# Joining two of the four exponentials of an attention step into one ScalarE instruction over two neighbouring PSUM banks

## The chip, the cores and the metric

The kernel runs on one core of one Trainium2 chip. The metric is the device time of one execution in microseconds, taken as the median of several runs. A core has a matrix engine (TensorE, in the profile PE, with its weight loads under PEld), a vector engine (VectorE, DVE), an engine for activation functions (ScalarE, ACT), a general engine (GpSimd, POOL) and an engine that mostly issues transfers (SyncE, SP). Matmuls write into PSUM, which has eight banks; one bank holds a tile of 128 rows by 512 fp32 numbers. ScalarE and VectorE read PSUM; GpSimd and the DMA queues do not.

## The reference

One block of a model: a layer norm without weights, an attention over 2048 tokens with 32 heads of 16 numbers each, a two-layer network with a tanh-approximated gelu on the same normed input, and a gated sum.

```
xn = layernorm(x)                        # x: 2048 x 512
q, k, v = split(xn @ wqkv)               # 32 heads of 16
p = softmax(q @ k.T * 16 ** -0.5)        # per head, 2048 x 2048
s = (p @ v) @ wo
h = gelu(xn @ w1 + b1)                   # 2048 x 1376
g = silu(h @ w2 + b2)
out = x + s * g
```

## The kernel before, in words

Most of the work is the attention. The kernel never stores the 2048 x 2048 scores of a head. It computes them twice. The first time (**S** operations) a tile of scores stands with the queries on the partitions, and VectorE takes the maximum of each row out of it (`s_mm`, `s_max`, L191). The second time (**T** operations, `t_one`, L715) it stands transposed, with the keys on the partitions, and the row maximum is subtracted inside the matmul by two extra rows of the operands; ScalarE takes the exponential out of PSUM into an SBUF tile (L717). A third matmul (`pv_step`, **V** in the order strings, L781) multiplies the exponentials by the values. To save precision, fp32 operands are split in a high and a low part; that is why the S operands have 48 rows (three pieces of 16) and the T operands 50.

An operand of 48 or 50 rows fills less than half of TensorE's 128 rows. So operands lie either in partitions 0 and up (row side 0, `a = 0`) or in partitions 64 and up (row side 1, `a = 1`), and two matmuls of different sides can run at the same time.

The work is cut in 32 units: 8 groups of 4 heads, times 4 chunks of 512 queries. A unit has 16 steps, one for each 128 keys. One step `n` (unit `ua`, key block `ka`) does for its 4 heads:

- four T matmuls and four exponentials, 128 x 512 each (T0 to T3 below);
- three S tiles, that run ahead of the T work by some units: two whole ones (`S`, the first on side 0, the next on side 1), and one tile written in two halves of 256 columns, `X` on side 0 and later `Y` on side 1, with a wait of TensorE's queue ahead of `Y` until `X` is done, since two row sides must not write one bank together. Each of the three gets one VectorE reduction;
- the V matmuls of the step before: 8 instructions, four column tiles in two passes each.

The order inside a step is written out by hand and kept by every engine's queue (`manual_schedule`): each letter issues its instructions in turn. A full step (three S tiles, `want == 3`) uses `TSXTTSTYV`, except `STXTTSTYV` at `ka` 0 and `XTSTTYSTV` at `ka` 2. There are 490 full steps, `n` 2 to 491; after them come 21 with no S (`TTTTV`), which also hold output work (`w_halves`, L905), and two odd ones at the start. Ahead of all this lies a first phase with the layer norm, the projections and the feed-forward network, into which the first S tiles are mixed.

PSUM has these users in a full step. The S ring (`ps_a`, `ps_b`, `ps_x`) has three banks that are handed round: S and X take the first one in the ring and put it at the end (X only when Y is issued). The T tiles rotate over `ps_m` and the three buffers of `ps_t` (`t_tile`). `ps_v` collects a unit's V result over 16 steps. At the end of a unit VectorE copies `ps_v` into SBUF (L788, tile `os`), which is issued behind the V of `ka` 0 of the next unit; the V of `ka` 1 writes `ps_v` anew. For two units at a time (later one) the maxima are turned by a TensorE transpose (`s_end1`, L268) into a T bank, copied out by VectorE (L278), and written to DRAM, from where they come back as the two extra rows of T.

Steps that the change and the prediction touch: `t_one` and `t_tile` (banks, row side, exponential), `pv_step` (the copy at L788), `s_end1` (the bank of the transpose), the order strings `ORDER` and `AFTER`, and the bank choice of the first phase and of the output (`a_tile`, `quad`, `down`, `w_mul`).

Of the kernel before, what the change touches and what calls it, by code (L numbers as in the profile page):

```python
# [8 lines left out]
F32 = mybir.dt.float32  # L9
F32R = mybir.dt.float32r  # L10
AF = mybir.ActivationFunctionType
OP = mybir.AluOpType
AX = mybir.AxisListType
PSUM = bass.MemoryType.PSUM
DRAM = bass.MemoryType.DRAM

P = 128
S = 2048
D = 512
# [3 lines left out]
NT = S // P  # L23
CH = 512
NCH = S // CH
# [5 lines left out]
SCALE = DH ** -0.5  # L31
VW = DH + 1
LEAD = 144
NW = 10
# [3 lines left out]
APART = 5  # L38
HB = 4
W2B = 2  # L40
ORDER = {0: "TTTTV", 3: "TSXTTSTYV"}
AFTER = {0: "STXTTSTYV", 2: "XTSTTYSTV"}
HC = CH // 2
PAIRED = 28
KB = 3
# [5 lines left out]
def fused(ctx: ExitStack, tc: tile.TileContext, x, wqk, wv, wo, w1, b1, w2, b2, out):  # L51
    nc = tc.nc
# [3 lines left out]
    ps_a = ctx.enter_context(tc.tile_pool(name="ps_a", bufs=1, space=PSUM))  # L56
    ps_b = ctx.enter_context(tc.tile_pool(name="ps_b", bufs=1, space=PSUM))
    ps_x = ctx.enter_context(tc.tile_pool(name="ps_x", bufs=1, space=PSUM))
    ps_t = ctx.enter_context(tc.tile_pool(name="ps_t", bufs=3, space=PSUM))
    ps_v = ctx.enter_context(tc.tile_pool(name="ps_v", bufs=1, space=PSUM))  # L60
    ps_m = ctx.enter_context(tc.tile_pool(name="ps_m", bufs=1, space=PSUM))

# [25 lines left out]
    SYNC = mybir.DependencyInfo(mybir.DependencyClass.Sync, mybir.DependencyReason.DATA)  # L88
    qss = []
    NU = NG * NCH  # L90

    s_ring = [ps_a, ps_b]

    def s_tile(held=False):
        pool = s_ring.pop(0)
        if not held:
            s_ring.append(pool)
        return pool.tile([P, CH], F32, name="ps"), pool
# [164 lines left out]
    prog = {}  # L263

    def s_end1(u):
        pm = s_tile()[0] if "seen" in prog or u == NU - 1 else t_tile()
        n = 2 * GH * NCH * len(units_of(u))
        nc.tensor.matmul(pm[:n, :P], NM.pop(u).rearrange("p u i a -> p (u i a)"), ident_r, start=True, stop=True)  # L268
        MH[u] = pm
# [122 lines left out]
    with ExitStack() as s1:  # L392
# [4 lines left out]
        def a_tile(shape):  # L397
            banks[0] += 1
            i = banks[0] % 6
            if i < 3:  # L400
                return (ps_a, ps_b, ps_x)[i].tile(list(shape), F32, name="ps")
            return ps_t.tile(list(shape), F32, name="pst")


        xs, xns = {}, {}
# [197 lines left out]
    PH = {}  # L603
# [21 lines left out]
    def down(c, f, part):  # L625
        i = c * FT + f
        if f == 0 and part == 0:
            PA[c] = [ps_v.tile([P, D], F32, name="pv")] + [ps_t.tile([P, D], F32, name="pst") for t in range(3)]
        h, w = HS[c, f], W2[c, f]
        side = (part + i) % 2  # L630
        ops = [[], []]
        for a in range(2):
            for t in ((0, 1), (2, 3))[(a + side) % 2]:
                ts = slice(t * P, (t + 1) * P)
                for n, (x, y) in enumerate(((0, 0), (0, 1), (1, 0))):
                    ops[a].append(((c, t), PA[c][t], h[x][:, ts], w[y],
                                   f == 0 and part == 0 and n == 0, f == FT - 1 and part == 1 and n == 2))
        run(ops)
        if part == 0:
            w2_split(i + 1)  # L640
            w2_load(i + 3)
            return
        del HS[c, f], W2[c, f]
        if f == FT - 1:
            for t in (0, 2, 1, 3):
                gt = wk.tile([P, D], F32, name="gt", bufs=4)
                if c == NCH - 1:
                    nc.vector.tensor_add(gt, PA[c][t], b2_sb)  # L648
                else:
                    nc.scalar.activation(gt, PA[c][t], AF.Copy)  # L650
                rs = slice(c * CH + t * P, c * CH + (t + 1) * P)
                if c < NCH - 1:
                    chores.append((gt, rs))
                else:
                    nc.gpsimd.dma_start(g_d[rs, :], gt)
# [22 lines left out]
    def quad(n, at):  # L678
        us = first[n]
        for u, b in zip(us, BANKS[n]) if at == 0 else ():  # L680
            pool, name = {"x": (ps_x, "ps"), "m": (ps_m, "ps"), "v": (ps_v, "pv"), "t": (ps_t, "pst")}[b]
            PH[u] = pool.tile([P, CH], F32, name=name)
        for i in range(at, at + 2):
            hooks = {}
            if n == VQ - 2 and i in (0, 2):
                hooks[3] = [lambda: w1_split(0) if i == 0 else w1_load(1)]
            run((terms(us[i], 0, i < 2), terms(us[(i + 2) % 4], 1, i < 2)), hooks)
            if i >= 2:
                for u in (us[i - 2], us[i]):
                    v_out(u[1] * NCH + u[2], PH.pop(u))  # L690
# [4 lines left out]
            errands.append((load_k, g, (i,)))  # L695

    PT = {}
    turns, PN = [0], []

    def t_tile():  # L700
        turns[0] += 1
        if turns[0] < 5:
            pool = (ps_m, ps_x, ps_a, ps_b)[turns[0] - 1]
        else:
            pool = ps_m if turns[0] % 4 == 1 else ps_t
        return pool.tile([P, CH], F32, name="pst" if pool is ps_t else "ps")

    def t_one(u, k, p, a):
        g = u // NCH
        if (u, k) not in PT:  # L710
            PT[u, k] = slot(3 + len(PN) % 3, (P, GH, CH))
            PN.append(1)
        ps = t_tile()
        r = slice(64 * a, 64 * a + 3 * DH + 2)
        nc.tensor.matmul(ps, kts[g % KB][p][r, k * P:(k + 1) * P],  # L715
                         QT[u][r, p, :], start=True, stop=True)
        nc.scalar.activation(PT[u, k][:, 2 * p + a, :], ps, AF.Exp, scale=SCALE)  # L717

    k_ones(kts[0])
    for n, e in enumerate(plan):  # L720
        if e[0] == "half":
            half(*e[1:])
        elif e[0] == "first":
            quad(*e[1:])
            if e[1:] == (0, 2):
                ask_qs(1)
        else:
            if e[1] == parts[-2]:
                nc.scalar.activation(mhw, ident_r[:1, :1].bitcast(F32), AF.Exp)
            if e[1] == parts[-1]:  # L730
                for i in range(EARLY):
                    t_one(0, 0, i // 2, i % 2)
            down(*e[1])
        if e == ("first", VQ - 1, 2):
            w2_split(0)
            w2_load(2)
            ask_k(1)
        if e[0] == "half" and pairs[e[1]][0] == ("q", NG - 1, 0) and e[2] == 1:
            kts.append([slot(p, (P, S), F32R) for p in range(2)])
            kws.append(None)  # L740
            qss.append(slot(2, (P, 2, 2, CH), F32R))
            ask_k(2)
        if n == len(plan) - 8:
            load_qt(0)
            load_mh(0)
# [29 lines left out]
    def pv_step(u, k):  # L775
        g = u // NCH
        if k == 0:
            PV[u] = ps_v.tile([P, CH], F32, name="pv")
        for j in range(GH):
            h = (g * GH + j) * VW  # L780
            nc.tensor.matmul(PV[u][32 * j:32 * j + 32, :], vsb[:, k, h:h + 32], PT[u, k][:, j, :],  # L781
                             start=(k == 0), stop=(k == NT - 1))
        del PT[u, k]
        if k == NT - 1:
            OS[u] = wb.tile([P, CH], F32, name="os", bufs=1)
            pv = PV.pop(u)
            if u < NU - 1:
                nc.vector.tensor_copy(OS[u], pv)  # L788
            else:
                nc.scalar.activation(OS[u][:, :HC], pv[:, :HC], AF.Copy)  # L790
                nc.vector.tensor_copy(OS[u][:, HC:], pv[:, HC:])
# [76 lines left out]

    def w_mul(t, ks, parts=(0, 1)):
        if t not in PW:  # L870
            PW[t] = [ps_t.tile([P, CH], F32, name="pst") if NW <= t < NT - NCH or i else
                     ps_m.tile([P, CH], F32, name="ps") if t == NT - 1 else s_tile()[0]
                     for i, cs in enumerate(cols(t))]
        for i, cs in enumerate(cols(t)):
            if i in parts:
                for k in ks:
                    mm3(PW[t][i][:, :cs.stop - cs.start], OTS[t, k], (wo_h[:, k, cs], wo_l[:, k, cs]),
                        k == 0, k == KT - 1)
# [97 lines left out]
    for n in range(L + 1):  # L976
        ua, ka = divmod(n, 16)
        want = due(n) - due(n - 1)
        i = 0
        for u in list(ended):  # L980
            if u >= PAIRED or ka > 2 and since.setdefault(u, n) < n:
                s_end0(u)
        order = ORDER[want] if n > 1 else ("TTTTV", "TTSTSVT")[n]
        if want == 3 and ua:
            order = AFTER.get(ka, order)
        for op in order:
            if op in "SXY":
                s_op(op)
            elif op == "V":
                if n:  # L990
                    pv_step(*divmod(n - 1, 16))
                for _ in range(4):
                    tick()
                flush()
            else:
                if EARLY <= 4 * n + i < 4 * L:
                    t_one(ua, ka, i % 2, 1 - i // 2)
                for f, args in todo.get((n, i), []):
                    f(*args)
                i += 1  # L1000
# [54 lines left out]
```

## Time and profile before

| | |
|---|---|
| median of 3 runs | 1565.8 us (1565.47 to 1566.19) |
| the profiled execution's own time | 1565.5 us |
| its span, first to last instruction | 1563.7 us |
| granted TensorE clock | 1.000 |
| first phase, to the first V | 470.39 us |
| the 490 full steps | 1007.94 us |
| steps after them, to the last V | 62.13 us |

How to read it: a busy time is the union of an engine's instruction times. An instruction's recorded time includes the way through its pipeline, so two instructions in a row overlap: four exponentials of about 0.60 us each follow one another at less than 0.50 us. An engine can therefore look busy without a gap and still have been held up; the distance from start to start tells more. "Idle before" names what ended an engine's idle time, and for a wait on several semaphores that is a guess.

### The profile page before, as it was taken

The numbers are of one execution on the slowest core, as the hardware profiler recorded it, in microseconds if no ns is written. First come the engines' busy times: TensorE is split into PE (matmuls) and PEld (weight loads), VectorE is DVE, ScalarE is ACT, GpSimd is POOL, SyncE is SP. The second block draws the span as 40 slices with busy tenths as digits, with TensorE's granted clock in tenths as the row PEclk, the third lists the DMA queues.
The fourth block names the chain that finished last, engine by engine and source line by source line (L and its number), as shares of the span: only waits on it lengthen the run. The fifth ranks groups of instructions, "written<-read, shape, count | busy, mean of one in ns | idle before, by whom it ended". The sixth has DMA issues, their size and how long they took to land.

```text
span 1563.7 us, 31870 instructions
## 1 busy us (share of the span) xinstructions
PE 1556.6 (100%) x12264; PEld 951.5 (61%) x12264; DVE 1416.1 (91%) x2290; ACT 1234.5 (79%) x2397; POOL 371.7 (24%) x394
## 2 busy tenths in 40 slices
PE   9999999999999999999999999999999999999998
PEld 7899999999994444444444444444444444444455
DVE  7599999999999999999999999999999999999834
ACT  4333333434349999999999999999999999999984
POOL 4145575756640011001100100100010000000143
PEclk9999999999999999999999999999999999999999
DMA  6626343454322113111511411321151111110163
GB/s 209 153 60 158 116 139 100 155 145 136 124 91 60 40 42 61 29 38 44 86 24 28 70 41 32 59 44 29 26 79 27 33 29 33 40 30 22 46 197 115
DMA packets 74648, 116.87 MB, mean 75 GB/s; under 512 B 23013, under 2 KB 24293, under 8 KB 73321
## 3 DMA queue, kind: packets, MB, share of 16 engines
q1 hardware_dynamic: 70748, 101.89, 23.9%
q0 software_dynamic: 3264, 12.35, 4.7%
q8 instruction: 97, 1.59, 0.4%
q10 hardware_dynamic: 484, 0.60, 0.1%
q14 instruction: 55, 0.44, 0.1%
HBM read 84.35 MB, written 25.97 MB: 71 GB/s over the span
## 4 chain that ended last, share of the span: by engine, by line
PE 98%; DVE 1%; ACT 0%; DMA 0%; issue 0%; DVEq 0%
PE pv L781 33%; PE pst L715 20%; PE ps L589 13%; PE ps L185 11%; PE pst L589 7%; PE ps L715 7%; PE pv L589 2%; PE ps L905 1%; PE ps L82 1%; PE ps L459 1%; PE pst L82 1%; DVE st L418 0%; PE pst L441 0%; DMA xt<-in_x 0%; PE pst L459 0%; ACT slot L717 0%
## 5 line engine op out<-in xcount | busy, mean ns | idle before, releaser
L191 DVE TENSOR_REDUCE mx<-ps 128x2 f32<-128x512 f32 x2048 | 1317.9, 687 | 87.2 <-PE ps L185 44.4
L717 ACT ACTIVATE slot<-pst 128x512 f32<-128x512 f32 x1533 | 826.0, 603 | 12.8 <-PE pst L715 7.0
L781 PE MATMUL pv<-slot,vsb 128*32 128x512 f32 x4096 | 545.4, 605 | 0.3 <-DVE os L788 0.3
L715 PE MATMUL pst<-qt,kt 50*128 50x512 f32 x1149 | 378.8, 430 | 0.5 <-DVE gt L648 0.3
L185 PE MATMUL ps<-kt,slot 48*128 48x512 f32 (+1 forms) x1364 | 377.1, 368 | 0.0
L715 PEld LDWEIGHTS pst<-qt,kt 50*128 50x128 f32 x1149 | 192.3, 185 | 252.5 <-ACT slot L717 235.9
L717 ACT ACTIVATE slot<-ps 128x512 f32<-128x512 f32 x515 | 310.9, 604 | 1.8 <-PE ps L185 0.7
L185 PEld LDWEIGHTS ps<-kt,slot 48*128 48x128 f32 x1364 | 226.6, 184 | 39.4 <-DVE mx L191 35.4
L589 PE MATMUL ps<-slot,w1h 64*128 64x512 f32 x1088 | 218.4, 393 | 0.0
L185 PE MATMUL ps<-kt,qz 48*128 48x512 f32 x512 | 201.8, 394 | 0.0
L185 PE MATMUL ps<-slot,slot 48*128 48x512 f32 (+1 forms) x598 | 165.3, 366 | 0.0
L715 PE MATMUL ps<-qt,kt 50*128 50x512 f32 x387 | 160.6, 417 | 0.0
L589 PEld LDWEIGHTS ps<-slot,w1h 64*128 64x128 f32 x1088 | 151.9, 186 | 10.5
L589 PE MATMUL ps<-slot,w1l 64*128 64x512 f32 x544 | 148.4, 393 | 0.0
L781 PEld LDWEIGHTS pv<-slot,vsb 128*32 128x32 f32 x4096 | 81.0, 108 | 98.9 <-issue 90.4
L378 POOL TENSOR_TENSOR hl<-hg,hh 128x512 fp32r<-128x512 f32 x76 | 96.8, 1296 | 151.9 <-ACT hh L377 113.9
L251 POOL CAST nmh<-nm 128x16 fp32r<-128x16 f32 x32 | 6.3, 197 | 519.4 <-DVE nm L248 418.0
L371 ACT ACTIVATE hg<-ps,b_sb 128x512 f32<-128x512 f32 x44 | 27.9, 684 | 125.2 <-PE ps L589 100.4
L715 PE MATMUL pst<-qt,slot 50*128 50x512 f32 x384 | 112.5, 416 | 0.0
L185 PEld LDWEIGHTS ps<-slot,slot 48*128 48x128 f32 x598 | 99.1, 184 | 16.4 <-DVE mx L191 15.1
L715 PEld LDWEIGHTS ps<-qt,kt 50*128 50x128 f32 x387 | 71.3, 185 | 41.8 <-ACT slot L717 36.0
L185 PEld LDWEIGHTS ps<-kt,qz 48*128 48x128 f32 x512 | 94.0, 184 | 0.5
(165 smaller groups left out, 1722.6 us busy)
## 6 DMA issues: line engine op xcount, KB each, us to landing
raw<-in_w SPq DMA_DIRECT2D x88, 256.0 KB
qk_h<-hh SPq DMA_DIRECT2D x32, 256.0 KB
qk_l<-hl SPq DMA_DIRECT2D x32, 256.0 KB
qt<-qk_h SPq DMA_DIRECT2D x128, 64.0 KB
slot<-qk_h SPq DMA_DIRECT2D x92, 64.0 KB
g_d<-gt POOLq DMA_DIRECT2D x16, 256.0 KB, 3.4
qt<-qk_l SPq DMA_DIRECT2D x64, 64.0 KB
dn<-den_d SPq DMA_DIRECT2D x32, 128.0 KB
```

Source lines behind the costliest of these rows:

```text
L82: nc.tensor.matmul(ps, lhs[a], rhs[b], start=first and n == 0, stop=last and n == 2)
L185: return nc.tensor.matmul(ps[:, c0:c0 + w], QS[u][r, p, qi * P:(qi + 1) * P], kts[u // NCH % KB][p][r, k0:k0 + w], start=True, stop=True).ins
L191: nc.vector.tensor_reduce(MX[u][:, 2 * p:2 * p + 2, qi, ki][:, heads, parts], ps.rearrange("p (n c) -> p n c", c=HC), axis=AX.X, op=OP.max)
L251: nc.gpsimd.tensor_copy(hl[:, 0], nm)
L371: nc.scalar.activation(raw, ph.pop(u), AF.Gelu_apprx_tanh, bias=b1_sb[:, u[2]:u[2] + 1])
L378: nc.gpsimd.tensor_sub(hl, raw, hh.bitcast(F32))
L459: nc.tensor.matmul(pq["q", g, c], W1[g][i][:, k * P:(k + 1) * P], (xh, xl)[j][c][:, k], start=n == 0 and k == 0, stop=n == 2 and k == KT - 1)
L589: i = nc.tensor.matmul(ps, lhs[r], rhs[r], start=first, stop=last).ins
L715: nc.tensor.matmul(ps, kts[g % KB][p][r, k * P:(k + 1) * P], QT[u][r, p, :], start=True, stop=True)
L717: nc.scalar.activation(PT[u, k][:, 2 * p + a, :], ps, AF.Exp, scale=SCALE)
L781: nc.tensor.matmul(PV[u][32 * j:32 * j + 32, :], vsb[:, k, h:h + 32], PT[u, k][:, j, :], start=(k == 0), stop=(k == NT - 1))
L905: HALF[0] = nc.tensor.matmul(PW[i][0], OTS[i, k][x][r], (wo_h, wo_l)[y][r, k], start=k == 0 and side == 0 and n == 0, stop=k == KT - 1 and ...
```

## The change

- The three `ps_t` buffers become one tile of two neighbouring banks (`two_t`, pool `ps_p`) and one single bank. `t_bank(i)` gives bank 0 or 1 of the pair, or the single one (2); without an argument it goes round the three. The places that took `ps_t` in the first phase and at the end take it from there.
- In full steps T1 goes to bank 0 and T2 to bank 1 of the pair, T0 to the single bank, T3 to `ps_m`. After T2, one ScalarE instruction takes the exponential of both banks, 128 x 1024, into the two neighbouring parts of the SBUF tile. T0 and T3 keep their own. For this the heads and row sides of the four T change: the sides were 1, 1, 0, 0 and are now 1, 0, 1, 0 (`SIDES`).
- All full steps use the order `XTSTTYSTV`.
- The copy of a unit's V result (L788) moves from VectorE to ScalarE, behind the last exponential of `ka` 0.
- The transpose of the maxima takes a bank of the S ring in place of a T bank.

```diff
-ORDER = {0: "TTTTV", 3: "TSXTTSTYV"}
-AFTER = {0: "STXTTSTYV", 2: "XTSTTYSTV"}
+ORDER = {0: "TTTTV", 3: "XTSTTYSTV"}
+SIDES = ((1, 1), (0, 0), (0, 1), (1, 0))
...
-    ps_t = ctx.enter_context(tc.tile_pool(name="ps_t", bufs=3, space=PSUM))
+    ps_t = ctx.enter_context(tc.tile_pool(name="ps_t", bufs=1, space=PSUM))
+    ps_p = ctx.enter_context(tc.tile_pool(name="ps_p", bufs=1, space=PSUM))
...
+    two_t = ps_p.tile([P, 2, CH], F32, name="two_t")
+    spare = [0]
+
+    def t_bank(i=None):
+        if i is None:
+            i = spare[0] % 3
+            spare[0] += 1
+        return two_t[:, i] if i < 2 else ps_t.tile([P, CH], F32, name="pst")
...
-        pm = s_tile()[0] if "seen" in prog or u == NU - 1 else t_tile()
+        pm = s_tile()[0]
...
-            PA[c] = [ps_v.tile([P, D], F32, name="pv")] + [ps_t.tile([P, D], F32, name="pst") for t in range(3)]
+            PA[c] = [ps_v.tile([P, D], F32, name="pv")] + [t_bank(i) for i in (0, 2, 1)]
...
-    def t_one(u, k, p, a):
+    def t_one(u, k, i, pair=False):
         g = u // NCH
+        p, a = SIDES[i]
...
-        ps = t_tile()
+        if u == k == 0:
+            ps = (ps_m, ps_x, ps_a, ps_b)[i].tile([P, CH], F32, name="ps")
+        elif i == 3:
+            ps = ps_m.tile([P, CH], F32, name="ps")
+        else:
+            ps = t_bank((i + 2) % 3)
...
-        nc.scalar.activation(PT[u, k][:, 2 * p + a, :], ps, AF.Exp, scale=SCALE)
+        if not pair or i in (0, 3):
+            nc.scalar.activation(PT[u, k][:, 2 * p + a, :], ps, AF.Exp, scale=SCALE)
+        elif i == 2:
+            nc.scalar.activation(PT[u, k][:, :2], two_t, AF.Exp, scale=SCALE)
...
-                nc.vector.tensor_copy(OS[u], pv)
+                nc.scalar.activation(OS[u], pv, AF.Copy)
...
-            PW[t] = [ps_t.tile([P, CH], F32, name="pst") if NW <= t < NT - NCH or i else
+            PW[t] = [t_bank(2 if t == NW else t == NW + 1) if NW <= t < NT - NCH or i else
...
-        if want == 3 and ua:
-            order = AFTER.get(ka, order)
...
-                    t_one(ua, ka, i % 2, 1 - i // 2)
+                    t_one(ua, ka, i, want == 3)
```

More of the change, by code (lines that the diff above doesn't have):

```diff
@@ L401, in a_tile @@
                 return (ps_a, ps_b, ps_x)[i].tile(list(shape), F32, name="ps")
-            return ps_t.tile(list(shape), F32, name="pst")
+            b = t_bank()
+            return b.rearrange("p (a b) -> p a b", b=shape[-1]) if len(shape) > 2 else b
         xs, xns = {}, {}
@@ L680, in quad @@
         for u, b in zip(us, BANKS[n]) if at == 0 else ():
-            pool, name = {"x": (ps_x, "ps"), "m": (ps_m, "ps"), "v": (ps_v, "pv"), "t": (ps_t, "pst")}[b]
-            PH[u] = pool.tile([P, CH], F32, name=name)
+            if b == "t":
+                PH[u] = t_bank()
+            else:
+                pool, name = {"x": (ps_x, "ps"), "m": (ps_m, "ps"), "v": (ps_v, "pv")}[b]
+                PH[u] = pool.tile([P, CH], F32, name=name)
         for i in range(at, at + 2):
@@ L697, in fused @@
     PT = {}
[L698 to L706, printed above, removed]
-    def t_one(u, k, p, a):
+    PN = []
+    def t_one(u, k, i, pair=False):
         g = u // NCH
+        p, a = SIDES[i]
         if (u, k) not in PT:
@@ L712, in t_one @@
             PN.append(1)
-        ps = t_tile()
+        if u == k == 0:
+            ps = (ps_m, ps_x, ps_a, ps_b)[i].tile([P, CH], F32, name="ps")
+        elif i == 3:
+            ps = ps_m.tile([P, CH], F32, name="ps")
+        else:
+            ps = t_bank((i + 2) % 3)
         r = slice(64 * a, 64 * a + 3 * DH + 2)
@@ L731, in fused @@
                 for i in range(EARLY):
-                    t_one(0, 0, i // 2, i % 2)
+                    t_one(0, 0, i)
             down(*e[1])
```

## The prediction

> **What bounds the kernel now.** I read the page first, for the engines and for the chain that ended last; then busy time by stage; then the timeline of single steps.
>
> ```profile
> PE 1556.6 (100%) x12264; PEld 951.5 (61%) x12264; DVE 1416.1 (91%) x2290; ACT 1234.5 (79%) x2397; POOL 371.7 (24%) x394
> ...
> PE 98%; DVE 1%; ACT 0%; DMA 0%; issue 0%; DVEq 0%
> ```
>
> The chain runs through TensorE nearly throughout. A gain must shorten what TensorE does or waits for; ScalarE time as such is worth nothing. The stage table (length, then busy time and count of PE, PEld, DVE, ACT, POOL) and the same stretch cut down to the V matmuls, the L278 copies and the L788 copies:
>
> ```profile
> 470.39:1478.33 1007.94, 1007.84 (x7856) 476.68 (x7855) 950.57 (x1567) 999.79 (x1961) 75.97 (x127) 1.00 0.20 41
> 470.39:1478.33 1007.94, 522.16 (x3920) 77.36 (x3921) 1.00 0.20 41
> 470.39:1478.33 1007.94, 3.56 (x13) 1.00 0.20 41
> 470.39:1478.33 1007.94, 20.44 (x30) 1.00 0.20 41
> ```
>
> 3920 V instructions, 8 to a step: 490 full steps of 2.057 us on average, with 13 transposes of maxima and 30 unit ends. All three engines look full, so the start times must tell. Two steps, each from T0 to the next T0 (start, length, instruction):
>
> ```profile
> 803.91 1.57 ACT L717 ACTIVATE slot<-pst 128x512 f32<-128x512 f32 x3
> 804.89 0.49 PE L715 MATMUL ps<-qt,slot 50*128 50x512 f32 x1
> 805.42 0.60 ACT L717 ACTIVATE slot<-ps 128x512 f32<-128x512 f32 x1
> 805.53 0.18 PEld L715 LDWEIGHTS pst<-qt,slot 50*128 50x128 f32 x1
> 805.91 1.57 ACT L717 ACTIVATE slot<-pst 128x512 f32<-128x512 f32 x3
> 805.95 1.07 PE L781 MATMUL pv<-slot,vsb 128*32 128x512 f32 x8
> 806.95 0.50 PE L715 MATMUL ps<-qt,slot 50*128 50x512 f32 x1
> 806.95 0.50 PE L185 MATMUL ps<-kt,slot 48*128 48x512 f32 x1
> 807.29 0.39 PE L715 MATMUL pst<-qt,slot 50*128 50x512 f32 x1
> 807.29 0.28 PE L185 MATMUL ps<-kt,slot 48*128 48x256 f32 x1
> 807.41 0.39 PE L715 MATMUL pst<-qt,slot 50*128 50x512 f32 x1
> 807.49 0.60 ACT L717 ACTIVATE slot<-ps 128x512 f32<-128x512 f32 x1
> 807.52 0.40 PE L185 MATMUL ps<-kt,slot 48*128 48x512 f32 x1
> 807.52 1.89 DVE L191 TENSOR_REDUCE mx<-ps 128x2 f32<-128x512 f32 x3 [0.18 <-PE ps L185]
> 807.53 0.18 PEld L715 LDWEIGHTS pst<-qt,slot 50*128 50x128 f32 x1
> 807.64 0.39 PE L715 MATMUL pst<-qt,slot 50*128 50x512 f32 x1
> 807.76 0.28 PE L185 MATMUL ps<-kt,slot 48*128 48x256 f32 x1
> 807.97 1.07 PE L781 MATMUL pv<-slot,vsb 128*32 128x512 f32 x8
> 807.98 1.57 ACT L717 ACTIVATE slot<-pst 128x512 f32<-128x512 f32 x3
> 808.96 0.50 PE L715 MATMUL ps<-qt,slot 50*128 50x512 f32 x1
> ```
>
> The reader is to see three things.
>
> *TensorE's own time.* A full T or S holds its row side 0.235 us (807.29 to 807.52; 807.41 to 807.64), a half one 0.12 (807.29 to 807.41). The first of a step costs 0.34 (806.95 to 807.29), so 0.105 is a start. V begins 0.095 after the last T has passed (807.64 + 0.235 to 807.97) and lasts 0.99 to 1.00. Undisturbed, T and S take 1.02 (806.95 to 807.97) and a step 2.01 to 2.02.
>
> *The slow step of the two.* The step at 804.89 needed 1.06. T3's weights are loaded at 805.53, 0.05 after the exponentials before it ended (803.91 + 1.57 = 805.48; a step later 805.91 + 1.57 = 807.48 and 807.53). T3 waits for its bank.
>
> *The loop through ScalarE.* T0 to its exponential 0.54, to the next three 0.49, these 1.57, release 0.05, T3's load to V 0.42, V 1.00: 4.07 us over two steps, which is 804.89 to 808.96. ScalarE's latency thus sets 2.035 a step, 0.02 above TensorE's own time.
>
> A second loop, through VectorE, is nearly as long: step start to the first reduction 0.57 (807.52), three reductions 1.89, release 0.05, then the last S tile to use that bank 0.105 + 0.235, Y behind it 0.12, 0.095 to V, V 1.00: 4.06.
>
> **The change, part by part.**
>
> *Joining.* 490 pairs. ScalarE's cost for size, same engine, bank and function:
>
> ```profile
> L390 ACT ACTIVATE vsb<-pv 128x512 f32<-128x512 f32 x2 | 1.2, 595 | 0.0
> L790 ACT ACTIVATE os<-pv 128x256 f32<-128x256 f32 x1 | 0.4, 385 | 1.0 <-PE pv L781 1.0
> ```
>
> 256 more elements cost 0.21 us, so 512 more cost 0.42. Single ones follow at (1.57 - 0.60) / 2 = 0.485, of which the rows after the first show 0.48. The pair holds ScalarE 0.90 instead of 0.96: 0.06 saved. The loop falls from 4.07 to 4.01, under TensorE's 4.03. No trace here shows a read over two banks: at best its fixed part vanishes as computed, at worst the pair takes two single ones' time and nothing is gained; I take 0.90, as the size rows are nearest.
>
> The Trainium skill ("ScalarE: Activation LUTs", What ACT_TABLE_LOAD costs) lets instructions with immediate scale and bias overlap by about 93 ns out of 186 ns fixed, and so would save 0.09. The rows give 0.06; by 0.09 the ScalarE loop is shorter still and the sum stays, as TensorE binds.
>
> *Later release of the pair.* T1 waits until the joined instruction ends: start of step + 0.54 + 0.49 + 0.90 + 0.12 = 2.05, released at 0.08 in the next step. T1's load is not due before 0.22. Costs nothing; without that cover each 0.01 costs 4.9 us.
>
> *Order and sides.* On side 0: X, S, T1, T3: 0.105 + 0.12 + 3 x 0.235 = 0.93. On side 1: T0, T2, Y, S: the same. Plus 0.095: 1.02, as now. But S starts 0.12 later, behind X, so the first reduction does too, while Y no longer stands behind the last S: the VectorE loop stays 4.06 as rounded, 2.03 a step. It lies between that and TensorE's 2.015; I take 2.02, nearer to the undisturbed step, since the old loop of 4.06 was itself never the limit. Before: (1007.94 - 30 x 0.17 - 13 x 0.28) / 490 = 2.039, with the two subtractions from here:
>
> ```profile
> 784.11 0.28 PE L268 MATMUL pst<-ident_r,nmh 128*64 128x128 f32 x1
> 784.32 0.50 PE L715 MATMUL ps<-qt,slot 50*128 50x512 f32 x1
> 785.41 1.07 PE L781 MATMUL pv<-slot,vsb 128*32 128x512 f32 x8
> ...
> 798.63 0.50 PE L715 MATMUL ps<-qt,slot 50*128 50x512 f32 x1
> 798.92 0.68 DVE L788 COPY os<-pv 128x512 f32<-128x512 f32 x1
> 800.70 0.39 PE L185 MATMUL ps<-kt,slot 48*128 48x256 f32 x1
> 800.86 0.18 PEld L185 LDWEIGHTS ps<-kt,slot 48*128 48x128 f32 x1
> 801.89 1.07 PE L781 MATMUL pv<-slot,vsb 128*32 128x512 f32 x8
> ```
>
> Full steps: 490 x (2.02 - 2.039) = -9.3 us.
>
> *Copy to ScalarE.* On VectorE it delays the reductions; `ka` 2 takes 1.19 (800.70 to 801.89) against 1.02: 0.17. On ScalarE, counted from the start of `ka` 0: last exponential at 1.93, copy at 2.41 (V ended at 1.02 + 1.07 = 2.09), next step's T0 exponential at 2.90 instead of 2.56, its pair at 3.39, its last one 4.29 to 4.90. T3 of `ka` 2 is released at 4.95, 0.91 into its step; + 0.42 is 1.33 against 1.02: 0.32 lost, not 0.17. Queued behind the copy: the exponentials alone; behind its result V of `ka` 1 (copy ends 3.01, V due 3.04) and the `o_move` transfers on SP's queue, which now wait to 0.99 in their step where they waited to 0.97 (798.92 + 0.68 against a step start of 798.63). 30 x 0.15 = +4.5 us.
>
> *Transposes.* Now 0.28 (784.11 to 785.41 is 1.30). In the S ring they take the first bank and shift the rest by one: the first S of the next step gets the bank of the last one, whose reduction ends 0.69 + 1.89 + 0.05 = 2.63 after step start, 0.61 after the transpose began; then three T or S and 0.095: 1.47 to 1.51, a loss of 0.47. 13 x 0.19 = +2.5 us.
>
> *Bank choice of the first phase and the end:* the same number of banks, freed by the same instructions; nothing. The 21 steps without S keep single exponentials.
>
> **Sum.** -9.3 + 4.5 + 2.5 = -2.3 us on the profiled 1565.5; the median of the runs is 0.3 higher, so 1563.5 us. A change of 0.2%, 3.1 us, is about what a measurement of this kernel can tell from none.
>
> **The rivals.**
>
> *The two side costs are hidden* (faster). If copy and transposes cost what they do now and the steps keep to 2.015, it is 490 x -0.024 = -11.8: 1554. For it: each rests on one bank's wait. Against: ScalarE's queue is in order, and the copy lies ahead of the exponentials.
>
> *The joined read saves nothing* (slower). Pair at 0.96: loop 4.07, 2.039 stays, only +7 remains: 1573. It decides from a pair of 0.95 on.
>
> *S behind X comes late every step* (slower). At 800.86 its weights are loaded 0.16 after the step's start, not 0.105, because the bank's reduction was late. Were that so in each step, T and S take 1.06 and a step 2.06: 490 x 0.02 + 7 = +17: 1583. Against: in an even flow that reduction ends 0.69 + 0.61 + 0.68 + 0.05 = 2.03 after the start before, 0.01 into the step. It decides at 0.10 more.
>
> *Row sides in strict order* (slower). T2 (side 1) stands behind T1 (side 0), which starts at 0.46. If a matmul could not start before an older one on the other side, T2 to Y to S end at 1.05 and V at 1.145: 490 x 0.125 is +61, so 1622 with the rest.
>
> ```profile
> 1513.88 0.49 PE L715 MATMUL pst<-qt,kt 50*128 50x512 f32 x1
> 1513.88 0.49 PE L905 MATMUL ps<-wo_h,oh 64*128 64x512 f32 x1
> 1514.21 0.39 PE L715 MATMUL pst<-qt,kt 50*128 50x512 f32 x1
> ```
>
> The program issues both T (the first two of a step without S, side 1) before this L905 (side 0), and the second T starts 0.33 later than it: no strict order. The Trainium skill ("TensorE: Matmul & The Clock Gate", The mechanism) states strict FIFO of starts; these rows differ, and the measurement decides.
>
> **How the numbers follow.** Forecast, 1560 to 1568: 0.45, of which 0.18 lies under 1562.7, more than 0.2% below the median. Hidden side costs, or part of them: 0.20. Joining saves nothing, or little: 0.19. Late S: 0.10. Strict order and the rest: 0.06. Hence faster 0.18 + 0.20 = 0.38, same 0.45 - 0.18 = 0.27, slower 0.35. The range 1554 to 1575 leaves out the last two cases, 0.16.
>
> **What would show it.** Right: exponentials of 128 x 1024 at about 1.02 us, the next one 0.90 after their start; T and S 1.02 in most steps; `ka` 2 longer by about 0.3, T3's load last; the first S late after each L268. Wrong: a full step of 2.04 (joining) or 2.06 (S's load past 0.105), T2 starting with T1 (order), or `ka` 2 at 1.02.

## The result, and the profile after

The changed kernel takes 1598.8 us (median of 4 runs, 1598.5 to 1601.8) against 1565.9 us before (4 runs, 1565.5 to 1566.2). The ratio is 1.021, with a 95% interval of 1.020 to 1.023: it is slower by 33 us. The forecast was 1563.5, with a range of 1554 to 1575.

The profiled execution took 1601.8 us, with a span of 1599.9 and a mean granted clock of 0.994; it is 3 us above the median, and differences of its stages are read with that in mind. Its page, first busy time by engine, then the shares of the chain that ended last, then the group of the joined instructions:

```profile
PE 1571.5 (98%) x12264; PEld 928.8 (58%) x12264; DVE 1398.9 (87%) x2259; ACT 1228.7 (77%) x1938; POOL 371.7 (23%) x394
...
PE 95%; ACT 3%; DVE 1%; issue 0%; DMA 0%; ACTq 0%; DVEq 0%
...
L732 ACT ACTIVATE slot<-two_t 128x1024 f32<-128x1024 f32 x490 | 503.4, 1027 | 0.3
```

The joined instruction was made 490 times and lasts 1.027 us. TensorE is busy for 98% of the span, not 100%, and ScalarE has appeared in the chain. So TensorE stands idle somewhere. The stages tell where (length, then busy time and count of PE, PEld, DVE, ACT, POOL, then the granted clock): the first phase, the 490 full steps, and the steps after them to the last V.

```profile
0.00:490.94 490.94, 476.85 (x3829) 434.34 (x3829) 429.90 (x674) 175.86 (x323) 261.18 (x241) 0.99 0.44 128
490.94:1498.95 1008.01, 1008.01 (x7855) 449.24 (x7854) 932.69 (x1535) 990.45 (x1501) 75.06 (x125) 1.00 0.20 40
1498.95:1576.76 77.81, 67.43 (x483) 30.69 (x481) 23.22 (x30) 58.56 (x111) 29.00 (x23) 1.00 0.41 138
```

The first and the last of these stages before:

```profile
0.00:470.39 470.39, 467.64 (x3829) 427.37 (x3829) 428.65 (x673) 175.12 (x322) 260.60 (x240) 1.00 0.46 132
1478.33:1540.46 62.13, 61.87 (x483) 32.83 (x482) 23.84 (x31) 55.76 (x111) 28.68 (x23) 1.00 0.54 172
```

| stage, us | before | after | difference |
|---|---|---|---|
| first phase, to the first V | 470.39 | 490.94 | +20.5 |
| 490 full steps | 1007.94 | 1008.01 | +0.1 |
| steps after, to the last V | 62.13 | 77.81 | +15.7 |

All the loss that the table shows lies in the two stages in which nothing is joined. The +0.1 of the full steps hides some more, though. Their first two, just behind the first phase, then the same two before:

```profile
490.94:498.25 7.31, 7.31 (x34) 3.38 (x33) 3.32 (x6) 3.97 (x7) 0.00 (x0) 0.53 0.31 99
```

```profile
470.39:475.02 4.63, 4.53 (x36) 2.02 (x34) 3.65 (x7) 3.74 (x8) 0.89 (x2) 1.00 0.59 213
```

They lose 2.7 us at a granted clock of 0.53, and the other 488 full steps together are 2.6 us shorter than before (1000.70 against 1003.31).

Of the 21 steps without S the last has only its V; 20 have T. In the last steps TensorE is now idle for 10.4 of 77.8 us. The timeline of a step there (start, length, instruction, and in brackets the idle time before it and what ended it):

```profile
1539.21 0.49 PE L727 MATMUL two_t<-qt,kt 50*128 50x512 f32 x1
1540.29 0.59 ACT L730 ACTIVATE slot<-two_t 128x512 f32<-128x512 f32 x1
1540.93 0.50 PE L727 MATMUL two_t<-qt,kt 50*128 50x512 f32 x1 [0.52 <-ACT slot L730]
1541.47 0.60 ACT L730 ACTIVATE slot<-two_t 128x512 f32<-128x512 f32 x1 [0.59 <-PE ps L727]
```

T1 is written into bank 0 of the pair at 1539.21 and read by its exponential from 1540.29 to 1540.88. T2 goes to bank 1 of the pair, which nobody reads at that time, and yet it starts only at 1540.93, 0.05 after that exponential's end. Then its own exponential follows. It waits as if for the tile `two_t`, not for the bank. The first phase shows the same, here with the transposes of the layer norm's output (`turn`, L452) and the splits that read them (L77, L78):

```profile
12.10 0.68 DVE L78 TENSOR_TENSOR slot<-two_t,slot 128x512 fp32r<-128x512 f32 x1
12.84 0.66 PE L452 MATMUL two_t<-ident,xn 128*128 128x128 f32 x4 [1.70 <-DVE slot L78]
13.54 0.60 ACT L77 ACTIVATE slot<-two_t 128x512 fp32r<-128x512 f32 x1 [1.69 <-PE two_t L452]
14.16 0.69 DVE L78 TENSOR_TENSOR slot<-two_t,slot 128x512 fp32r<-128x512 f32 x1 [1.38 <-ACT slot L77]
```

TensorE stands 1.70 us, until the VectorE instruction on the pair has ended at 12.78, and each engine waits for the one before it in the list. The view of waits adds these up (us in total, times, longest), first for the whole run, then for the last steps alone:

```profile
PE two_t L727 <- ACT slot L730: 10.8, 21, 0.9
PE two_t L452 <- DVE slot L78: 9.6, 4, 2.7
```

```profile
PE two_t L727 <- ACT slot L730: 10.4, 20, 0.9
```

20 of the 21 waits on ScalarE, one for each of the 20 steps with T and without S, make 10.4 us, which is all of TensorE's idle time there; the other lies in step 1, which is not joined either. The remaining 5.3 us of that stage's loss lie in instructions that count as busy and were not taken apart. The four waits of 9.6 us are the direct part of the first phase's loss. Another part shows in stretches of 25 us from the start: TensorE is not only idle, the clock granted to it falls.

```profile
25.00:50.00 25.00, 22.28 (x89) 18.06 (x88) 14.99 (x39) 6.73 (x14) 3.93 (x4) 0.82 0.35 119
50.00:75.00 25.00, 21.71 (x123) 17.14 (x123) 2.60 (x4) 8.97 (x16) 5.05 (x4) 0.93 0.78 194
```

In 25 to 50 us there are 89 matmuls at a clock of 0.82; before, the same 25 us held 127 at 1.00:

```profile
25.00:50.00 25.00, 25.00 (x127) 20.61 (x125) 14.43 (x37) 13.21 (x26) 5.10 (x4) 1.00 0.66 197
```

From the third on, the full steps look as they were forecast. An ordinary one, from T0 to the next T0:

```profile
818.96 0.50 PE L727 MATMUL pst<-qt,slot 50*128 50x512 f32 x1
819.98 1.06 PE L796 MATMUL pv<-slot,vsb 128*32 128x512 f32 x8
819.99 1.02 ACT L732 ACTIVATE slot<-two_t 128x1024 f32<-128x1024 f32 x1
820.89 0.61 ACT L730 ACTIVATE slot<-ps 128x512 f32<-128x512 f32 x1
820.97 0.39 PE L195 MATMUL ps<-kt,slot 48*128 48x256 f32 x1
```

T and S take 1.02 (818.96 to 819.98), the step 2.01. T3's exponential begins 0.90 after the joined one. And a unit's end:

```profile
821.37 0.62 ACT L803 ACTIVATE os<-pv 128x512 f32<-128x512 f32 x1
822.33 1.07 ACT L732 ACTIVATE slot<-two_t 128x1024 f32<-128x1024 f32 x1
823.04 0.39 PE L195 MATMUL ps<-kt,slot 48*128 48x256 f32 x1
823.23 0.66 ACT L730 ACTIVATE slot<-ps 128x512 f32<-128x512 f32 x1
823.94 0.18 PEld L727 LDWEIGHTS ps<-qt,slot 50*128 50x128 f32 x1
824.36 1.07 PE L796 MATMUL pv<-slot,vsb 128*32 128x512 f32 x8
```

The copy lies ahead of the exponentials on ScalarE, the last exponential ends at 823.89, T3's weights are loaded at 823.94, 0.90 into the step of `ka` 2, and V starts 1.32 into it.

### The profile page after: what moved, and what is told of

Same layout as the page of the kernel before. It is cut to its first block, busy times and chain, and to the rows that moved or that the text cites. A ratio compares the mean times of both kernels' runs of the same rounds, so it can differ in the third digit from the quotient of the medians.

```text
span 1599.9 us, 31404 instructions
## 1 busy us (share of the span) xinstructions
PE 1571.5 (98%) x12264; PEld 928.8 (58%) x12264; DVE 1398.9 (87%) x2259; ACT 1228.7 (77%) x1938; POOL 371.7 (23%) x394
## 4 chain that ended last, share of the span: by engine, by line
PE 95%; ACT 3%; DVE 1%; issue 0%; DMA 0%; ACTq 0%; DVEq 0%
PE pv L796 31%; PE ps L195 21%; PE ps L600 12%; PE two_t L727 8%; PE two_t L600 5%; PE ps L727 4%; PE pst L727 4%; PE pst L600 2%; PE pv L600 2%; ACT slot L730 2%; PE ps L83 1%; PE ps L470 1%; PE ps L920 1%; ACT slot L732 1%; PE two_t L83 0%; PE pst L83 0%
## 5 line engine op out<-in xcount | busy, mean ns | idle before, releaser
L732 ACT ACTIVATE slot<-two_t 128x1024 f32<-128x1024 f32 x490 | 503.4, 1027 | 0.3
L195 PEld LDWEIGHTS ps<-kt,slot 48*128 48x128 f32 x1364 | 213.9, 184 | 289.4 <-DVE mx L201 278.1
L195 PE MATMUL ps<-kt,slot 48*128 48x256 f32 (+1 forms) x1364 | 373.7, 363 | 0.0
L730 ACT ACTIVATE slot<-pst 128x512 f32<-128x512 f32 x511 | 308.6, 604 | 23.6 <-PE two_t L727 7.2
L730 ACT ACTIVATE slot<-ps 128x512 f32<-128x512 f32 x515 | 315.6, 613 | 1.8 <-PE pst L727 1.8
L727 PE MATMUL two_t<-qt,kt 50*128 50x512 f32 x766 | 208.5, 406 | 11.5 <-ACT slot L730 10.8
L727 PE MATMUL pst<-qt,kt 50*128 50x512 f32 x383 | 190.4, 497 | 0.5 <-DVE gt L659 0.5
L195 PEld LDWEIGHTS ps<-slot,slot 48*128 48x128 f32 x598 | 94.8, 186 | 128.4 <-DVE mx L201 123.4
L195 PE MATMUL ps<-slot,slot 48*128 48x256 f32 (+1 forms) x598 | 164.8, 365 | 0.0
L727 PEld LDWEIGHTS two_t<-qt,kt 50*128 50x128 f32 x766 | 112.9, 186 | 23.9 <-ACT slot L730 20.0
```

Source lines behind the costliest of these rows:

```text
L195: return nc.tensor.matmul(ps[:, c0:c0 + w], QS[u][r, p, qi * P:(qi + 1) * P], kts[u // NCH % KB][p][r, k0:k0 + w], start=True, stop=True).ins
L727: nc.tensor.matmul(ps, kts[g % KB][p][r, k * P:(k + 1) * P], QT[u][r, p, :], start=True, stop=True)
L732: nc.scalar.activation(PT[u, k][:, :2], two_t, AF.Exp, scale=SCALE)
```

## The experiments

The theory: waits on the pair are kept for the tile. A matmul into one of its banks waits for the readers of the other one, in the first phase and in the last 21 steps; the full steps are right as forecast. The rivals: the other edits (order, sides, copy, transposes) cost the time; or the joined instruction does.

**The pair as one tile only where it is joined.** `e1_apart` opens two single tiles for the first phase, one tile of two banks for the full steps, and two single tiles again for the last 21. `e2_first_phase_apart` leaves the last part out.

```diff
-    two_t = ps_p.tile([P, 2, CH], F32, name="two_t")
+    ps_1 = [... .tile_pool(name=f"ps_{c}", bufs=1, space=PSUM) for c in "pq"]
...
+        if i < 2 and not two_t:
+            return ps_1[i].tile([P, CH], F32, name="pst")
...
     s_ring.append(ps_x)
+    to_pair()
     qz.close()
...
+        if n == DONE:
+            to_single("rs")        # not in e2
```

> The changed kernel, but the pair of banks is one tile only during the full steps; in the first phase, and again in the 21 steps without S and the output, its two banks are two separate tiles. Theory A (a matmul into one bank of the pair waits for the readers of the other bank, because the wait is kept for the whole tile): first V back from 490.9 to about 470.5 us, the 21 last steps back from 77.8 to about 62.1 us, the full steps stay at about 1008 us, the median falls by 33 to about 1565 us, no change against the kernel before. Rival B (the loss comes from the new row sides and bank order in those stages, or from a lower clock that the run happened to have): the two stages stay as they are, above 1590 us.

> As the run before this one, but only the first phase has separate tiles; from the full steps on the pair stays one tile. Theory A: first V at about 470.5 us, last 21 steps still 77 to 78 us, time about 1581 us. Rival B: first V stays at about 490 us.

Measured: `e1_apart` 1567.1 us (10 runs, 1565.2 to 1569.0), ratio to before 1.001 (1.000 to 1.002), so 32 of the 33 us are gone. `e2_first_phase_apart` 1583.9 (one run). The last steps of the first, then those of the second:

```profile
1480.65:1542.58 61.93, 61.93 (x484) 32.40 (x482) 23.22 (x30) 56.14 (x111) 28.67 (x23) 1.00 0.53 174
```

```profile
1480.50:1558.38 77.88, 67.51 (x484) 30.76 (x482) 23.19 (x30) 58.57 (x111) 28.94 (x23) 1.00 0.41 138
```

With single tiles they take 61.93 us, with the pair 77.88, with the same `t_bank` numbers and the same order. The first phase falls to 473.0 and 472.5, not quite to the 470.5 expected; the changeover (below) holds the rest. The clock in 25 to 50 us is back at 1.00 in `e1_apart`, with TensorE busy throughout:

```profile
25.00:50.00 25.00, 25.00 (x126) 20.60 (x126) 14.38 (x37) 13.26 (x26) 5.11 (x4) 1.00 0.64 192
```

So the clock's fall came with the waits and went with them. What it cost beside them was not measured apart; an estimate from the two rows of the changed kernel, 25 x 0.18 + 25 x 0.07, is some 6 of the 20.5 us.

**The pair alone, in the kernel before.** `e3_before_with_pair_first` makes two of the three T buffers of the first phase one tile, and nothing else; from the first step on it is the kernel before.

```diff
+    two_t = ps_p.tile([P, 2, CH], F32, name="two_t")
...
+        return two_t[:, i] if i < 2 else ps_1.tile([P, CH], F32, name="pst")
...
     s_ring.append(ps_x)
+    pair_stack.close()
+    ps_t = ctx.enter_context(tc.tile_pool(name="ps_t", bufs=3, space=PSUM))
     qz.close()
```

> The kernel before, with the one part added: in the first phase two of the three rotating banks are one tile; from the first full step on three separate banks as before, no joining, old order. Theory A: first V at 487 to 491 us, granted clock under 1 in the first 100 us, time 1583 to 1587 us, full steps unchanged at 1008 us. Rival B: 1566 us, first V at 470 us.

Measured: 1584.0 us (one run), 18.7 above the runs of before beside it (1565.3). Its first phase:

```profile
0.00:486.50 486.50, 472.50 (x3830) 428.44 (x3830) 430.43 (x674) 175.35 (x322) 261.17 (x241) 0.99 0.44 129
```

It is 16.1 us longer than before. The pair costs this without any of the other edits. The full steps, expected unchanged, took 1010.5 us, 2.6 more than before: the first three of them took 9.29 us at a mean clock of 0.63, where before took 6.69 at 1.00.

The Trainium skill ("PSUM — Partial Sum Buffer", PSUM bank collisions raise a hardware error) asks for a semaphore by bank and by quadrant of partitions where two engines meet. By that rule T2 in bank 1 needs no wait for a reader of bank 0, and the single tiles, which run without it, agree. The program's waits on a tile of two banks were wider than the rule.

**What the joining itself is worth.** `e4_no_joining` keeps the new order, sides, copy and transposes, with four single exponentials and single tiles throughout.

```diff
-                    t_one(ua, ka, i, want == 3)
+                    t_one(ua, ka, i, False)
```

> New order, new row sides, copy on ScalarE, transpose in the S ring, but four single exponentials in every step and separate banks everywhere. By the loop through ScalarE of the prediction (4.07 us for two steps without joining, 4.01 with it) an ordinary full step takes 2.035 to 2.04 us where the joined one takes 2.015: 490 x 0.02 = 10 us more than e1_apart, about 1575 us. Rival C (the new order alone brings the step to 2.015, joining does nothing): the same time as e1_apart within 2 us.

Measured: 1575.8 us (4 runs, 1575.4 to 1577.3), ratio 1.007 (1.005 to 1.008), 8.7 above `e1_apart`. But `e1_apart` also loses some 3 us at the changeover to the pair, which `e4_no_joining` never makes. The run that differs from it in joining alone is `e9_late_pair` (below): 1564.0 us, so joining is worth 11.8 us, and of this 11.7 lie in the full steps (1017.05 against 1005.36). Two full steps without joining in its timeline:

```profile
818.73 1.07 PE L812 MATMUL pv<-slot,vsb 128*32 128x512 f32 x8
820.74 1.06 PE L812 MATMUL pv<-slot,vsb 128*32 128x512 f32 x8
...
821.71 0.62 ACT L746 ACTIVATE slot<-ps 128x512 f32<-128x512 f32 x1
...
822.38 0.18 PEld L743 LDWEIGHTS ps<-qt,slot 50*128 50x128 f32 x1
...
822.80 0.64 PE L812 MATMUL pv<-slot,vsb 128*32 128x512 f32 x4
```

The steps alternate again between 2.01 (818.73 to 820.74) and 2.06 (to 822.80), as in the kernel before, and in the slow one T3's weights come 0.05 after the exponential before has ended (822.33 and 822.38). With the joined instruction all ordinary steps take 2.01 to 2.02; without it, the loop through ScalarE binds.

**The copy of V's result.** Three runs ask what its new place costs. `e5_copy_on_dve` puts it back on VectorE; `e6_copy_split` gives half the columns to each engine; `e8_before_copy_split` does the same in the kernel before.

```diff
-                nc.scalar.activation(OS[u], pv, AF.Copy)
+                nc.vector.tensor_copy(OS[u], pv)                               # e5
...
+                nc.scalar.activation(OS[u][:, :HC], pv[:, :HC], AF.Copy)       # e6, e8
+                nc.vector.tensor_copy(OS[u][:, HC:], pv[:, HC:])
```

> e1_apart with the copy of a unit's V result back on VectorE. Theory D (the copy costs what it delays on the engine that carries it: on ScalarE T3 of ka 2 is released 0.3 us late): on VectorE the 0.60 us stand ahead of the first S reduction, of which about 0.22 us is idle time; the last S tile of ka 2 is then late by about 0.37 us, so ka 2 takes 2.35 to 2.40 us, ka 1 falls from 2.06 to about 2.02, and the time stays that of e1_apart within 3 us. Rival E (the 2.32 us of ka 2 do not come from the copy): ka 2 stays at 2.32 with its wait on ScalarE.

> e1_apart with the copy halved: columns 0 to 255 on ScalarE, 256 to 511 on VectorE. Theory D: ScalarE is held up 0.26 instead of 0.48 us, VectorE 0.33 against 0.22 us idle; both loops come out about 0.11 us late, so ka 2 takes about 2.13 us and ka 1 about 2.02: 30 x 0.24 = 7 us less than e1_apart, about 1560 us, faster than the kernel before. Rival E: ka 2 stays at 2.32, no gain.

> The kernel before with the copy halved over ScalarE and VectorE alone. If e7 gains by joining, this one gains little: VectorE's 0.17 us at ka 2 fall to about 0.05, but ScalarE, whose loop binds here, is held up 0.26 us: between 1562 and 1567 us. If the halved copy alone carries the gain, it comes to 1558 us or less.

Measured: `e5_copy_on_dve` 1566.8 us (10 runs), no different from `e1_apart`. On VectorE the cost is spread: `ka` 1 and 2 take 2.172 and 2.222 us, not the 2.02 and 2.35 to 2.40 expected, against 2.062 and 2.324 with ScalarE; the sums agree (4.394, 4.386). `e6_copy_split` 1571.6 us (4 runs, 1569.3 to 1573.5), 4.6 worse than `e1_apart` where 1560 was expected, and `e8_before_copy_split` 1575.9 (4 runs), 10 worse than before. The timeline of `e6_copy_split` at a unit's end:

```profile
802.55 0.41 ACT L820 ACTIVATE os<-pv 128x256 f32<-128x256 f32 x1
...
802.99 0.42 DVE L821 COPY os<-pv 128x256 f32<-128x256 f32 x1 [0.31 <-ACT os L820]
...
803.47 1.06 PE L813 MATMUL pv<-slot,vsb 128*32 128x512 f32 x8 [0.23 <-DVE os L821]
```

The halves do not run side by side. VectorE stands 0.31 us and starts 0.03 after ScalarE's half has ended (802.96), and V, which writes that bank anew, waits for it. `ka` 1 and 2 take 2.31 and 2.22 us, together 0.14 more than in `e1_apart`; over 30 units that is 4.3 us. In `e8_before_copy_split` VectorE stands 0.52 us in the same way, `ka` 1 takes 2.37 us in place of 2.06, and V waits too. Both halves read one bank and write one tile; which of the two made VectorE wait was not told apart. Both expectations were wrong for this reason. The trace of before could have told it: its last unit already splits this copy, and there, too, VectorE's half (L791) starts at 1542.87 us, 0.03 after ScalarE's half (L790) has ended.

**The changeover.** `e1_apart` spread over 3.8 us from run to run, where before spreads over 1.5. Ten microseconds of its trace at the first steps, where the pair is one tile already but steps 0 and 1 are not joined, and below the same ten of `e11_changeover`:

```profile
470.00:480.00 10.00, 8.86 (x41) 3.71 (x45) 4.37 (x8) 4.98 (x9) 1.35 (x3) 0.66 0.49 152
```

```profile
470.00:480.00 10.00, 9.67 (x73) 4.27 (x75) 8.32 (x15) 8.50 (x15) 1.86 (x5) 1.00 0.49 154
```

In the first the clock is 0.66, and 41 matmuls are done against 73. The first two full steps of `e1_apart` take 6.88 us against 4.63 before. `e7_split_and_late_pair` (with the split copy) and `e9_late_pair` (without) open the pair from step 2 only; `e10_joined_to_the_end` is `e9_late_pair` with the last 20 steps that have T joined as well; `e11_changeover` also deals step 1's banks in the order in which they come free.

```diff
-    to_pair()                      # at the changeover
+        if n == 2:                 # e7, e9, e10, e11
+            to_pair()
...
-                    t_one(ua, ka, i, want == 3)
+                    t_one(ua, ka, i, n > 1)          # e10, without to_single
...
-        elif i == 3:
+        elif i == 3 * (u > 0 or k > 1):              # e11
             ps = ps_m.tile([P, CH], F32, name="ps")
+        elif u == 0 and k == 1:
+            ps = t_bank((2, 0, 1)[i - 1])
```

> e6_copy_split, and the pair becomes one tile only at step 2, where joining begins, so that step 1 with its single exponentials has separate banks too. Theory A: steps 0 and 1 in e1_apart lose 4.5 us between 468 and 479 us by waits of one bank of the pair on the other; these go, about 1555 us, 0.65% faster than the kernel before. Rival B: the same time as e6_copy_split.

> e1_apart (copy whole on ScalarE), with the pair made one tile only at step 2. Theory A: step 1 loses its false waits, 2 to 4.5 us less than e1_apart: 1563 to 1565 us. In e7 the clock still halved for 6.8 us at the changeover; if it does so here, nearer to 1565.

> e9_late_pair, but in place of separate banks after the full steps the 21 last steps join their exponentials too and keep the pair as one tile. Theory A: where both banks are read by one instruction there is no reader of the neighbour to wait for, so these steps take 3.05 us as with separate banks; the same time as e9_late_pair within 2 us. Rival B (the new row sides cost in these steps): 3.85 us a step, 16 us more.

> e9_late_pair, and the first T of step 1 goes to ps_m, which no sum of the first phase holds, as in the kernel before; T1, T2, T3 follow in the order in which VectorE frees the three other banks. Theory F (the clock halves between 472 and 479 us because TensorE stands for 0.5 us and then works on one row side alone, which comes from T0 waiting for the second of these banks): clock 1.00 throughout, first V at 470.5 us, 3 to 4 us less than e9_late_pair, about 1561 us, 0.3% faster than the kernel before, and less spread between runs. Rival G (the clock falls for another reason): still about 0.5 there, the time of e9_late_pair.

| kernel | median, us (runs) | from, to | ratio to before (95%) |
|---|---|---|---|
| before | 1565.7 (27) | 1564.9, 1566.4 | |
| `e7_split_and_late_pair` | 1569.0 (7) | 1567.6, 1571.1 | 1.002 (1.001 to 1.004) |
| `e9_late_pair` | 1564.0 (10) | 1563.7, 1567.1 | 0.9992 (0.9983 to 1.0001) |
| `e10_joined_to_the_end` | 1564.1 (10) | 1563.6, 1565.5 | 0.9990 (0.9981 to 0.9999) |
| `e11_changeover` | 1563.8 (11) | 1563.3, 1564.5 | 0.9988 (0.9979 to 0.9997) |

The row of before is that of the last three; `e7_split_and_late_pair` ran beside 17 runs of before with the same median. `e7_split_and_late_pair` missed its 1555 by the split copy. The others agree with each other; against `e1_apart`, `e9_late_pair` has 471.6 us of first phase for 473.0 and 1005.4 of full steps for 1007.6. Joining these last steps, with the pair kept, is worth nothing and costs nothing: the pair does no harm as one tile where it is read as one. `e11_changeover` came out below before by 0.1%, not the 0.3% expected of it. It has the lowest median here and the least spread of these four, but 0.2 us below `e9_late_pair` is within the noise: `e9_late_pair` kept its clock at 1.00 in the profiled run and in eight others, so there was little left to gain. That the order of `e11_changeover` keeps the clock up is not shown (no run of 11 lost it, against one of 10). Its full steps:

```profile
470.83:1476.38 1005.55, 1005.22 (x7856) 447.84 (x7855) 932.81 (x1536) 990.33 (x1501) 75.71 (x127) 1.00 0.20 41
```

They take 1005.55 us. The forecast for them, with the copy and the transposes, was 1007.94 - 2.3 = 1005.6. The agreement is closer than that of the parts, and so in part luck (next section).

## Why the prediction was wrong

*The step that failed* is "Bank choice of the first phase and the end: the same number of banks, freed by the same instructions; nothing." The number of banks is the same, but they are not freed by the same instructions. Once two buffers are one tile, each bank is freed by the readers of both. In the first phase this costs 16 to 18 us (`e3_before_with_pair_first` +16.1 alone; 490.9 against 472.5 in `e2_first_phase_apart`), and some 2 more at the changeover, up to the +20.5 of the changed kernel. The first two full steps lose 2.7 at half clock, which single tiles in step 1 mostly avoid (`e9_late_pair`), and the last steps 15.7 (20 times 0.78). Less the 2.6 gained in the other full steps, the stages sum to 36 in the profiled run, whose own time stands 36 above the profiled one of before. The prediction asked about the joined instruction's own release of the pair and found it covered, in full steps alone; it did not ask it of the stages where the pair is used bank by bank. No rival had this mechanism.

*Joining* was right. The joined read lasts 1.027 us where 1.02 was forecast, the next one starts 0.90 later as forecast, ordinary steps take 2.01 to 2.02 as forecast (2.02), and without joining 11.8 us are lost, where the sum had 9.3. The sizes inside the sum differ and offset each other: the ordinary step is 2.015 rather than 2.02, which is 490 x 0.005 = 2.4 us more gain; `ka` 1, at which the prediction saw no loss, takes 2.064, which is 30 x 0.05 = 1.5 less.

*Later release of the pair* in full steps costs nothing, as said: they would not be at 2.015 else.

*The copy* was right in size: 0.31 lost in `ka` 2 where 0.32 was forecast, T3's load 0.90 into the step where 0.91 was. That VectorE would have kept it cheaper was wrong: with the new order `e5_copy_on_dve` costs the same. The +4.5 us were thus no price of the engine: with this order of the step and the pair joined, either engine pays the same.

*The transposes* lose 0.34 to 0.46 (steps of 2.36 to 2.48 against 2.016) where 0.47 was forecast.

*The rivals.* S late at each step and strict order of the row sides were wrong: the one would have shown ordinary steps of 2.06, the other longer ones. That the side costs are hidden was wrong, by `ka` 2. That the joined read saves nothing was wrong, by `e4_no_joining`. The slower side came about by a way that was not among them.

The whole loss of the changed kernel is then told: with the waits by tile taken away, the rest of the change gives 1564.0 us (`e9_late_pair`; 1563.8 with step 1's banks in order), where the sum was 1563.5. That is 0.1% below before: the gain in the steps is nearly given back by the copy and the transposes.

## What to carry to other kernels

When two buffers become one tile, so that an instruction can read both, ask for each place that still uses them singly who reads the other half: waits may be kept for the tile. Make them one tile only for the stage in which they are read as one, and single tiles elsewhere. A stage that a change seems only to rename deserves its own line in the forecast, with one instruction of it followed from write to release.

## What the runs showed of the hardware

One ScalarE instruction over two neighbouring PSUM banks works at the same rate as over one: 1.027 us for 1024 columns, with the next one 0.90 later, against 0.60 and 0.48 for 512. Against two single reads that saves 0.06 (2 x 0.48 - 0.90).

The clock granted to TensorE can fall to half after a short disturbance. In the profiled run of `e7_split_and_late_pair` TensorE stood 0.52 us at the changeover, and matmuls then came sparsely (its timeline, then single microseconds by the clock in the third column from the end):

```profile
469.95 1.09 PE L743 MATMUL pst<-qt,kt 50*128 50x512 f32 x2 [0.52 <-DVE gt L675]
```

```profile
474.00:475.00 1.00, 1.00 (x7) 0.94 (x5) 0.35 (x1) 0.99 (x2) 0.00 (x0) 0.50 0.04 16
480.00:481.00 1.00, 1.00 (x12) 0.74 (x8) 0.65 (x3) 0.63 (x2) 0.41 (x2) 1.00 0.07 18
```

The clock is 0.50 at 474 us and 1.00 at 480. The Trainium skill ("TensorE: Matmul & The Clock Gate", Part 1: The HAM clock gate) gives an idle window of about 3.4 us before the clock falls to half. The half clock agrees; the rows show no stand of that length, here or in the first phase of the changed kernel, where the longest wait of TensorE on the pair was 2.7. What exactly sets it off was not tested. The same program falls or does not: three of the seven runs of `e7_split_and_late_pair` have a mean clock of 0.997 (1570.5 to 1571.1 us), the other four 1.000 (1567.6 to 1569.0), and in `e9_late_pair`, which differs from it only in the copy, nine runs of ten kept 1.000. The runs of `e1_apart` lie between 1565.2 us at a mean clock of 1.000 and 1569.0 at 0.997, while those of `e11_changeover` stay at 0.999 to 1.000 and within 1.1 us.
